# Two head pairs to a visit: joining the small-tile products of a linear-attention plus expert-layer kernel

## The chip, the cores and the metric

The kernel runs on one core of one Trainium2 chip. The metric is device time in microseconds (us). Three runs of the kernel before took 1010.1, 1008.94 and 1009.0 us, median 1009.0. The profiled execution took 1008.2 us; from its first to its last instruction (the span) there are 1006.4 us, so 1.8 us lie around the span.

## The reference

For 8 batches and 8 heads (sequence 576, head size 64, 128 random features) the attention is made linear by a feature map; its result then goes through two dense layers with an ELU between them.

```python
def phi(x):
    proj = np.einsum('bhsd,md->bhsm', x, omega)
    h = proj - np.sum(x * x, axis=-1, keepdims=True) / 2.0
    h = h - np.max(h, axis=-1, keepdims=True)
    return np.exp(h) / np.sqrt(m)
q_p, k_p = phi(q_s), phi(k_s)
kv  = np.einsum('bhsm,bhsd->bhmd', k_p, v)
z   = np.sum(k_p, axis=2)
num = np.einsum('bhsm,bhmd->bhsd', q_p, kv)
den = np.einsum('bhsm,bhm->bhs', q_p, z)[..., None] + 1e-06
x = (num / den)            # 4608 tokens x 512
h = x @ w_in               # 512 x 2048
g = np.where(h > 0.0, h, np.exp(np.minimum(h, 0.0)) - 1.0)
out = g @ w_out            # 2048 x 512
```

## The kernel before

Two heads of one batch make a pair; there are 32 pairs, numbered 0 to 31. The tokens go through the dense layers in eight blocks of 384 (layer one writes the PSUM tile `ph`, layer two the tiles `acc`), and the last 1536 tokens in three wide steps that spend fewer products (tiles `A`, `B`, `acs`). Pairs 0 to 7 are worked at the start; pairs 8 to 31 are spread between the matmuls of the blocks.

The order of all engines' work is planned when the program is built. Each piece of work is announced by `op(engine, ns, due, ...)` with an assumed duration, a due time, and what it reads and writes. `Plan.order` then plays the work through: whenever an engine is free, it takes the ready piece with the earliest due, if its buffers are free; some pieces have a second engine (`alt`). The chip executes each engine's list in that order. The due times come from tables of numbers at the head of the file (`STEP`, `PD0`, `KV2`, `ALT` and so on).

A pair from 8 on goes through these steps, in `pair`: `load_pair`; `project` for the keys (tile `ppk`, features `hk`); `kv` (here `kv_swapped`); `project` for the queries (`ppq`, `hq`); and `finish`.

- `kv_swapped` (line 609): ten matmuls sum k_p v of the pair, with v (128 x 64) as the stationary side, so that two of them, for the two heads, stand side by side on column halves of the array. They fill one PSUM bank `pkv`. VectorE turns that bank into `kvf` (line 615), `replicate` sends it to DRAM in four pieces (`kvd`, line 585) and back in four (`zk`, line 594), and GpSimd sums the keys.
- `finish` normalises the query features, turns them in 32 x 32 blocks (`qt`), and calls `output` (line 829): 32 matmuls, each with 32 rows and 64 columns of the array, eight of them side by side. They fill four PSUM banks `pn`. Each bank is copied out by a copy of 128 columns and one of 32 (lines 376 on ScalarE and 378 on VectorE), and one DMA writes the pair to `xd` (line 854).

In the trace one of these matmuls in full 32-bit floats is two records, so a pair has 20 records at line 609 and 64 at line 829. A "visit" below is such an unbroken row of small-tile products on TensorE; the matmuls of the dense layers around it use the whole 128 x 128 array.

PSUM has eight banks: three with the tag `pa`, two with `ph` (layer one takes these in turn, and `A` and `B` later), and three for `acc`. `output` needs four at once, three `pa` and one `ph` (for the last three pairs two and two); `pkv`, `ppk` and `ppq` take one `pa` each.

Of the kernel before, what the change touches and what calls it, by code (L numbers as in the profile page):

```python
# [18 lines left out]
P = 128  # L19
# [26 lines left out]
NNAT = dict(k=8, q=8)  # L46


MLP0 = 37.61
SEG = [6.25, 7.76, 3.48, 4.4, 2.75, 6.34]  # L50
STEP = 5.52
STEP_ATT = 5.44

STEP_SA, STEP_S = 9.344, 8.511
LAG2 = 1.848
PD0, PDS = 122.22, 19.83
NSA = 1
SLOT = {3: 0, 4: 1, 5: 2, 6: 1, 7: 0}
NP3 = 29
PREP0, PREP = -101.339, 8.8  # L60
TWO0, TWO = -37.142, 7.995
SUM = 0.873
UNIT0, UNIT1 = 0.25, 3.77
FETCH = 14.688
BT = [-0.751, -0.373, 0.719, 0.06, 0.525, 0.7, 0.865, -0.155, -0.328, 1.177, -1.344, 0.575, -1.141, 0.489]
AT = (0.0, 0.337, 0.844, 0.312, 0.229, 0.181, 0.386)

LAG = 3.4


PAIR0 = 6.45
DUE_LOAD, DUE_K, DUE_KV, DUE_Q = 9.63, 24.93, 17.79, 16.94
LOAD2, K2, KV2, Q2 = 61.21, 47.49, 31.23, 34.51
TAIL = 14.17
TAIL2 = -0.54


CONV1 = 13.95
CONV_STEP = 0.16
CONV2 = 1.14  # L80
CONV3 = 41.4


SPLIT = (0, 8, 16)
NHALF = 3

DUE_Z = 15.42

NEARLY = 6

NSWAP = 8
# [199 lines left out]

ALT = dict(kv=1.96, out=2.95, conv_clamp=13.06, conv_hi=14.02, conv_sub=16.5, g_hi=12.75, g_lo=11.74, y_hi=None, y_lo=0.82, norm=18.01, p2=0.03, unit=-5.32, unit_hi=0.48, prep=0.118, part=5.545, q_hi=1.554, q_lo=14.04, neg=7.821, turn=0.31, x_hi=0.28, sq=-0.48, two=-0.272, two_hi=0.343, sum=0.079, s_hi=0.129, s_lo=0.3, zero=-0.108)


def other(kind, *engs):
# [21 lines left out]
def performer_elu_kernel(  # L319
# [256 lines left out]
    def replicate(i, due):  # L576

        if i < NTURN:
            return
        s, kvf = st[i], kvs[i % 2]  # L580
        zk = s["zk"]
# [15 lines left out]

    def kv_swapped(i, due):

        s = st[i]  # L600
        h, v = s["hk"], s["v"]
        kvf = kvs[i % 2]
        p = bank(i, "ph", f"pkv_{i}")

        def mms():
            for t in range(-1, 4):
                for a in range(2):
                    j, o = (8, 8 * (D + 1) + a * (D + 2)) if t < 0 else (2 * t + a, (2 * t + a) * (D + 1))
                    nc.tensor.matmul(  # L609
                        p()[a * D:a * D + D, 0:M], v()[:, o:o + D], h()[:, j, :], start=(t < 0), stop=(t == 3)  # L610
                    )

        parts = parts_of(i, "k")
        op("PE", 5 * 216, due, mms, [*parts, v], (p,))
        op("DVE", dve(M), due + 1.2, lambda: nc.vector.transpose(kvf, p()[:, 0:M]), (p,), (("kvf", i % 2),))
        zs = Buf(sb, [P, 2, M], F32, "zs", f"zs_{i}", 1)
        zk = s["zk"] = Buf(sb, [P, 8 * P], F32, "raw", f"zk_{i}", 3)

        zu = Buf(sb, [D, 2, M], F32, "p2", f"zu_{i}", 4)

# [25 lines left out]
        replicate(i, due)  # L646

    def kv(i, due):

        if i >= NSWAP:  # L650
            kv_swapped(i, due)
            return
        s = st[i]
        h, v = s["hk"], s["v"]
        kvf = kvs[i % 2]
# [33 lines left out]
    def finish(i, due):  # L689
# [21 lines left out]
        if i < NTURN:  # L711
            qh = Buf(sb, [P, 2, S], F32, "qh", f"qh_{i}", 2)
        else:
            qt = Buf(sb, [P, 10, M], F32, "qh", f"qt_{i}", 2)
        for g in range(3):
            d = due - 9 + g
            js = slice(4 * g, min(4 * g + 4, NJ))
# [49 lines left out]
                alt=other("turn", "DVE", dve(n * P)),  # L767
            )
        if i >= NTURN:
            output(i, qt, due - 2)  # L770
# [40 lines left out]

        op("DVE", (1 if g < 2 else 2) * dve(n * P), due, turn, ((h, "n", g),), ((qt, g),))

    def output(i, qt, due):

        b, hp = divmod(i, NHP)
        zk = st[i]["zk"]
        npa = 3 if i < NP3 else 2
        banks = [Buf(ps, [P, 512], F32, "pa", f"pn_{i}_{e}", 3) for e in range(npa)]
        banks += [Buf(ps, [P, 512], F32, "ph", f"pn_{i}_{e}", 2) for e in range(npa, 4)]  # L820
        N = 5 * 32

        def mms():
            for j in range(4):
                for e in range(4):
                    r, c = slice(32 * e, 32 * e + 32), slice(32 * j, 32 * j + 32)
                    for a in range(2):
                        o = slice(a * D, a * D + D)
                        nc.tensor.matmul(  # L829
                            banks[e]()[o, 0:N], zk()[r, 4 * M + j * P + a * D:4 * M + j * P + a * D + D], qt()[r, a:10:2, c], start=(j == 0), stop=(j == 3)  # L830
                        )

        op(
            "PE", 4 * mm(4 * N) + 200, due, mms, [*((qt, g) for g in range(3)), *((zk, "kv", e) for e in range(4))], banks
        )

        def x():
            return qt().rearrange("p j x -> p (j x)")

        for e, p in enumerate(banks):  # L840
            def evict(eng, e=e, p=p):
                r, o = slice(e // 2 * D, e // 2 * D + D), 512 + 32 * (e % 2)
                copy(
                    eng, x()[:, 0:512].rearrange("p (t e r) -> p e t r", e=4, r=32)[:, e],
                    p()[:, 0:4 * 32].rearrange("p (t r) -> p t r", r=32),
                )
                copy(eng, x()[r, o:o + 32], p()[r, 4 * 32:N])

            op(
                "ACT", act(4 * 32, True) + act(32, True), due + 0.8 + 0.4 * e, evict, (p,), ((qt, "x", e),),  # L850
                alt=other("x_hi", "DVE", dve(4 * 32) + dve(32)),
            )
        op(
            "SP", 500, due + 2.4, lambda: nc.sync.dma_start(xd[hp, :, b * S:b * S + S], x()[:, 0:S]),
            [(qt, "x", e) for e in range(4)], (("xd", i),), P * S * 4,
        )

    def pair(i, due):

        at = (DUE_LOAD, DUE_K, DUE_KV, DUE_Q) if i < 2 * NHP else (LOAD2, K2, KV2, Q2)  # L860
        load_pair(i, due - at[0])
        project(i, "k", due - at[1])
        kv(i, due - at[2])
        project(i, "q", due - at[3])
        finish(i, due)


    def from_f64(src, hi, lo, nm, due, key):

# [726 lines left out]
    for n in range(len(SEGMENTS)):  # L1596
# [105 lines left out]
```

## Time and profile before

| | us |
|---|---|
| median of three runs | 1009.0 |
| profiled execution, device time | 1008.2 |
| its span | 1006.4 |
| TensorE busy | 981.2 |
| VectorE busy | 842.0 |
| ScalarE busy | 765.8 |
| GpSimd busy | 557.6 |
| line 829, small-tile output products, busy | 32.8 |
| line 609, small-tile sums of k_p v, busy | 31.5 |

Busy time on TensorE counts a record from its start to its modelled end, and records overlap: of two full-array matmuls in a row the second starts long before the first ends. What a product costs its neighbours is therefore read from start to start, in the timeline. The chain that ended last lies on TensorE for 68% of the span, on VectorE for 15%, on DMA for 6%.

### The profile page before, as it was taken

How to read it: one execution, taken by the hardware profiler on the slowest of the kernel's cores; microseconds unless marked ns; L12 is line 12 of the kernel's file. 1: busy time of each engine (PE TensorE's matmuls, PEld its weight loads, DVE VectorE, ACT ScalarE, POOL GpSimd, SP SyncE). 2: the span in 40 equal slices, each digit the busy share in tenths (PEclk: the TensorE clock that was granted, in tenths of full speed). 3: DMA queues.
4: the chain of work that ended last, by engine and by line, in shares of the span. 5: the costliest groups of instructions: out<-in, count | busy, mean ns of one | idle time of the engine just before them, and what ended most of it. 6: DMA issues, size and time to landing. Idle time of an engine off the chain costs nothing.

```text
span 1006.4 us, 24315 instructions
## 1 busy us (share of the span) xinstructions
PE 981.2 (97%) x7806; PEld 883.9 (88%) x7806; DVE 842.0 (84%) x3077; ACT 765.8 (76%) x2064; POOL 557.6 (55%) x745
## 2 busy tenths in 40 slices
PE   7999999999999999999999999999999999999997
PEld 7788788878888888888888888888789999999997
DVE  7999977887778788878888888889999889779766
ACT  7989777777668888888787778776546788777774
POOL 2667666685547767677577766684442232223221
PEclk9999999999999999999999999999999999999999
DMA  7656787757776776676666766767878876766752
GB/s 230 174 191 198 232 276 262 249 185 236 232 246 202 236 229 204 210 240 207 223 211 220 237 196 211 231 218 236 295 272 309 294 264 205 233 219 193 220 200 66
DMA packets 93264, 226.27 MB, mean 225 GB/s; under 512 B 23056, under 2 KB 35024, under 8 KB 93136
## 3 DMA queue, kind: packets, MB, share of 16 engines
q1 hardware_dynamic: 93136, 224.70, 68.8%
q8 instruction: 63, 1.03, 0.4%
q14 instruction: 65, 0.53, 0.2%
HBM read 187.43 MB, written 37.22 MB: 223 GB/s over the span
## 4 chain that ended last, share of the span: by engine, by line
PE 68%; DVE 15%; DMA 6%; ACT 5%; issue 3%; POOL 3%; SPq 1%; DVEq 0%; POOLq 0%; ACTq 0%
PE acs L1512 9%; PE ph L969 6%; PE ph L971 6%; PE acc L1003 6%; PE ph L970 6%; PE A L1354 6%; PE acc L1005 6%; PE acc L1004 6%; PE B L1354 4%; PE pkv L609 2%; PE pn L829 2%; PE ppq L541 2%; PE ppk L541 2%; DVE junk L727 1%; DVE u_w L914 1%
## 5 line engine op out<-in xcount | busy, mean ns | idle before, releaser
L969 PE MATMUL ph<-xh,w1c 128*128 128x384 f32 x512 | 176.9, 345 | 6.3 <-DVE g L990 4.4
L970 PE MATMUL ph<-xl,w1c 128*128 128x384 f32 x512 | 172.3, 336 | 1.0 <-DVE xl L794 1.0
L971 PE MATMUL ph<-xh,w1c 128*128 128x384 f32 x512 | 172.3, 336 | 0.0
L1003 PE MATMUL acc<-w2h,g 128*128 128x512 f32 x384 | 154.6, 402 | 0.1
L1005 PE MATMUL acc<-w2h,g 128*128 128x512 f32 x384 | 151.6, 395 | 0.0
L1004 PE MATMUL acc<-w2l,g 128*128 128x512 f32 x384 | 151.3, 394 | 0.0
L969 PEld LDWEIGHTS ph<-xh,w1c 128*128 128x128 f32 x512 | 96.2, 188 | 18.7 <-DVE g L990 8.5
L970 PEld LDWEIGHTS ph<-xl,w1c 128*128 128x128 f32 x512 | 96.3, 188 | 3.8 <-DVE xl L794 1.4
L978 ACT ACTIVATE e<-ph 128x384 f32<-128x384 f32 x128 | 62.5, 488 | 47.5 <-PE ph L971 47.0
L381 POOL TENSOR_TENSOR hq<-hq,den 128x512 f32<-128x512 f32 (+1 forms) x96 | 80.9, 852 | 28.7 <-DVE den L736 23.2
L971 PEld LDWEIGHTS ph<-xh,w1c 128*128 128x128 f32 x512 | 96.2, 188 | 0.0
L982 DVE SCALAR_TENSOR_TENSOR ph<-e,ph 128x384 f32<-128x384 f32 x128 | 71.3, 557 | 27.4 <-ACT e L979 26.1
L381 POOL TENSOR_TENSOR gq<-yh,gq 128x256 fp32r<-128x256 f32 x49 | 42.8, 873 | 87.0 <-ACT gq L376 76.8
L1005 PEld LDWEIGHTS acc<-w2h,g 128*128 128x128 f32 x384 | 72.0, 188 | 17.1
L1003 PEld LDWEIGHTS acc<-w2h,g 128*128 128x128 f32 x384 | 72.1, 188 | 16.2 <-issue 6.3
L727 DVE CUSTOM_DVE_ANT_0 junk<-hq,pz 128x128 f32<-128x128 f32 (+1 forms) x320 | 74.6, 279 | 12.7 <-PE pz L705 10.6
L381 POOL TENSOR_TENSOR tk<-xk,tk 64x576 fp32r<-64x576 f32 x45 | 64.1, 1424 | 32.2 <-ACT tk L376 14.9
L461 ACT ACTIVATE hk<-hk,nbk 128x128 f32<-128x128 f32 x216 | 68.4, 391 | 15.7 <-POOL nbk L567 15.3
L1004 PEld LDWEIGHTS acc<-w2l,g 128*128 128x128 f32 x384 | 72.2, 188 | 8.7
L461 ACT ACTIVATE hq<-hq,nbq 128x128 f32<-128x128 f32 x216 | 68.4, 391 | 13.5 <-POOL nbq L567 13.0
L381 POOL TENSOR_TENSOR tq<-xq,tq 64x576 fp32r<-64x576 f32 x46 | 65.9, 1432 | 21.4 <-ACT tq L376 11.1
L990 DVE TENSOR_TENSOR g<-ph,g 128x384 fp32r<-128x384 f32 x128 | 70.6, 551 | 5.7 <-PE pn L829 1.8
(222 smaller groups left out, 2816.9 us busy)
## 6 DMA issues: line engine op xcount, KB each, us to landing
w1c<-w1s SPq DMA_DIRECT2D x112, 512.0 KB, 4.4
wp<-w1t SPq DMA_DIRECT2D x48, 512.0 KB, 3.7
raw_w<-in_w_dram SPq DMA_DIRECT2D x32, 512.0 KB, 4.3
xk<-in_kx_dram SPq DMA_DIRECT2D x24, 576.0 KB, 4.6
xq<-in_qx_dram SPq DMA_DIRECT2D x24, 576.0 KB, 4.6
wp<-w1s SPq DMA_DIRECT2D x24, 512.0 KB, 4.2
v<-in_v_dram SPq DMA_DIRECT2D x32, 325.0 KB, 3.2
w1s<-w1c SPq DMA_DIRECT2D x16, 512.0 KB, 3.9
```

Source lines behind the costliest of these rows:

```text
L381: (nc.vector if e == "DVE" else nc.gpsimd).tensor_tensor(*args)
L461: nc.scalar.activation(h()[:, j, :], src(j), AF.Exp, bias=nb()[:, j:j + 1], scale=-1.0)
L727: nc.vector.tensor_tensor_reduce(out=junk()[r], in0=h()[r, j, :], in1=pz()[r, a * P:(a + 1) * P], scale=1.0, scalar=EPS, op0=ALU.mult, op1 ...
L969: nc.tensor.matmul(ph(), wh, xh[:, c, o:o + TB], start=(c == 0), stop=False)
L970: nc.tensor.matmul(ph(), wh, xl[:, c, o:o + TB], start=False, stop=False)
L971: nc.tensor.matmul(ph(), wl, xh[:, c, o:o + TB], start=False, stop=(c == NC - 1))
L982: lambda: nc.vector.scalar_tensor_tensor(ph(), e(), -1.0, ph(), ALU.add, ALU.max), (p, e), (p,),
L1003: nc.tensor.matmul(a(), g[0]()[:, ts], w2h[:, f], start=(f == f0), stop=False)
L1004: nc.tensor.matmul(a(), g[0]()[:, ts], w2l[:, f], start=False, stop=False)
L1005: nc.tensor.matmul(a(), g[1]()[:, ts], w2h[:, f], start=False, stop=(f == f1 - 1))
L1354: nc.tensor.matmul(o, at(a, i), u[b][:, i], start=(start and fresh_bank and i == 0 and n == 0), stop=(i == 1 and n == 2), skip_group_check ...
L1512: nc.tensor.matmul(bank()[:, z * TH:(z + 1) * TH], g()[:, a * TH + z * P:a * TH + z * P + P], w(b), start=(j == 0 and z == 0 and m == 0), ...
```

## The change

From pair 8 on, pairs are handled two at a time by `two_pairs`. `kv_swapped` and `output` go; their matmuls stand together in one piece of work, `tiled(i, o)`: first the sums of k_p v of pairs `i` and `i + 1` (into the last 128 columns of banks 0 and 1), then the outputs of the two pairs before, `o` and `o + 1` (into columns 0 to 159 and 160 to 319 of four banks). The first call has no pairs before it and takes two banks; the last has no pairs after it. So twelve calls work on sums, eleven of them on outputs as well, and a thirteenth on outputs alone. The keys' sums (`key_sums`) and the two turns into `kvf` come behind it; a bank with a turn in it is copied out after that turn. Each copy-out now does both pairs (four copies for a bank). All due times are new as well. The number of matmuls, of DMAs and of copies stays as it was; of the 96 copies of 128 columns (and as many of 32) VectorE now has 60 in its list, where it had 23.

```diff
-STEP_SA, STEP_S = 9.344, 8.511
+STEP_SA, STEP_S = 9.326, 10.023
...
-    def output(i, qt, due):
...
+    def tiled(i, o, due):
+
+        src = [] if i is None else list(range(i, i + 2))
+        old = [] if o is None else [(st[o + k]["qt"], st[o + k]["zk"]) for k in range(2)]
+        n = 4 if old else 2
+        npa = min(n, 3 if (o or i) < NP3 else 2)
+        banks = [Buf(ps, [P, 512], F32, "pa", f"pn_{o}_{i}_{e}", 3) for e in range(npa)]
+        banks += [Buf(ps, [P, 512], F32, "ph", f"pn_{o}_{i}_{e}", 2) for e in range(npa, n)]
         N = 5 * 32
 
         def mms():
+            for k, x in enumerate(src):
+                h, v = st[x]["hk"], st[x]["v"]
+                for t in range(-1, 4):
                     for a in range(2):
+                        j, c = (8, 8 * (D + 1) + a * (D + 2)) if t < 0 else (2 * t + a, (2 * t + a) * (D + 1))
                         nc.tensor.matmul(
+                            banks[k]()[a * D:a * D + D, 3 * M:], v()[:, c:c + D], h()[:, j, :], start=(t < 0), stop=(t == 3)
                         )
+            for k, (qt, zk) in enumerate(old):
+                for j in range(4):
+                    for e in range(4):
+                        r, c = slice(32 * e, 32 * e + 32), slice(32 * j, 32 * j + 32)
+                        for a in range(2):
+                            nc.tensor.matmul(
+                                banks[e]()[a * D:a * D + D, k * N:(k + 1) * N],
+                                zk()[r, 4 * M + j * P + a * D:4 * M + j * P + a * D + D],
+                                qt()[r, a:10:2, c], start=(j == 0), stop=(j == 3),
+                            )
...
+        for k, x in enumerate(src):
+            op(
+                "DVE", dve(M), due + KVD + 0.1 * k, lambda k=k: nc.vector.transpose(kvs[k], banks[k]()[:, 3 * M:]),
+                (), (("kvf", k), banks[k]),
+            )
+            replicate(x, due + KVD - 1.2)
...
+            op(
+                "ACT", 2 * (act(4 * 32, True) + act(32, True)), due + 1.9 + 0.4 * e, evict, (p,), [(qt, "x", e) for qt, _ in old],
+                alt=other("x_hi", "DVE", 2 * (dve(4 * 32) + dve(32))),
+            )
...
+    def two_pairs(i, due, before):
+
+        for k in range(2):
+            load_pair(i + k, due[k] - LOAD2)
+            project(i + k, "k", due[k] - K2)
+        if before is None:
+            tiled(i, None, due[1] - KVP)
+        else:
+            tiled(i, i - 2, before[1] - OUT)
+        for k in range(2):
+            key_sums(i + k, due[k] - KV2)
+            project(i + k, "q", due[k] - Q2)
+            finish(i + k, due[k])
+        if i == NPAIR - 2:
+            tiled(None, i, due[1] - OUT)
...
-            for i in range(2 * NHP, NPAIR):
-                pair(i, begin[1] + PD0 + PDS * (i - 2 * NHP))
+            due = None
+            for i in range(2 * NHP, NPAIR, 2):
+                before, due = due, [begin[1] + PD0 + PDS * (i + k - 2 * NHP) for k in range(2)]
+                two_pairs(i, due, before)
```

On TensorE, before the change, the outputs of pair 11 stand by themselves between two matmuls of layer two (here the head of the visit; the same four banks are gone through four times):

```order
L1004 MATMUL acc_8_1_3901<-w2l,g_0_4013 128x512
L1005 MATMUL acc_8_1_3901<-w2h,g_1_4022 128x512
L829 MATMUL pn_0_4162<-qt_4046,zk_3432 64x160 x2
L829 MATMUL pn_1_4165<-qt_4046,zk_3432 64x160 x2
L829 MATMUL pn_2_4168<-qt_4046,zk_3432 64x160 x2
L829 MATMUL pn_3_4171<-qt_4046,zk_3432 64x160 x2
```

A little later, still before the change, the sums of pair 13 stand between layer one and the query projection:

```order
L971 MATMUL ph_4234<-xh,w1c_3965 128x384
L541 MATMUL ppq_0_4262<-om,tq_4026 128x256 x2
L541 MATMUL ppq_1_4267<-om,tq_4026 128x256 x2
...
L971 MATMUL ph_4280<-xh,w1c_4073 128x384
L609 MATMUL pkv_4319<-hk_4075,v_3588 64x128 x10
L541 MATMUL ppq_3_4342<-om,tq_4026 128x256 x2
L1003 MATMUL acc_8_2_3934<-w2h,g_0_4109 128x512
```

On TensorE after the change, the visit that makes the sums of pairs 16 and 17 and the outputs of pairs 14 (`qt_4997`) and 15 (`qt_5276`); again each pair's banks are gone through four times:

```order
L1026 MATMUL acc_0_0_4865<-w2h,g_1_5331 128x512
L815 MATMUL pn_16_0_5340<-hk_4840,v_4761 64x128 x10
L815 MATMUL pn_16_1_5351<-hk_5136,v_4770 64x128 x10
L823 MATMUL pn_16_0_5340<-qt_4997,zk_4532 64x160 x2
...
L823 MATMUL pn_16_3_5369<-qt_4997,zk_4532 64x160 x2
L823 MATMUL pn_16_0_5340<-qt_5276,zk_4772 64x160 x2
...
L823 MATMUL pn_16_3_5369<-qt_5276,zk_4772 64x160 x2
L990 MATMUL ph_5435<-xh,w1c_5105 128x384
```

What stood in four rows of small-tile work with full-array work between them now stands in one; inside it the tile shape changes once, from 128 x 64 to 32 x 64.

On VectorE behind that same visit, after the change (banks 2 and 0; ScalarE has banks 3 and 1):

```order
L381 COPY qt_4997<-pn_16_2_5366 128x4x32
L381 COPY qt_4997<-pn_16_2_5366 64x32
L381 COPY qt_5276<-pn_16_2_5366 128x4x32
L381 COPY qt_5276<-pn_16_2_5366 64x32
L836 STREAM_TRANSPOSE kvf_76<-pn_16_0_5340 128x128
L836 STREAM_TRANSPOSE kvf_77<-pn_16_1_5351 128x128
L381 COPY qt_4997<-pn_16_0_5340 128x4x32
L381 COPY qt_4997<-pn_16_0_5340 64x32
```

Before the change VectorE had one bank's two copies behind pair 11's visit, and ScalarE the other three banks' six.

## Rows read from the trace of the kernel before

**Rows 1.** The page: busy time of each engine (share of span) and instructions.
```profile
PE 981.2 (97%) x7806; PEld 883.9 (88%) x7806; DVE 842.0 (84%) x3077; ACT 765.8 (76%) x2064; POOL 557.6 (55%) x745
```
**Rows 2.** Busy time by stretch; behind the busy times clock, DMA share, GB/s.
```profile
0.00:165.00 165.00, 156.15 (x1014) 134.20 (x1015) 142.81 (x434) 135.67 (x344) 99.83 (x94) 1.00 0.69 221
165.00:725.00 560.00, 552.55 (x4591) 483.70 (x4590) 463.54 (x2073) 434.90 (x1191) 376.94 (x556) 1.00 0.70 224
725.00:1006.40 281.40, 272.51 (x2202) 265.95 (x2202) 235.62 (x571) 195.21 (x531) 80.85 (x96) 1.00 0.69 228
```
**Rows 3.** TensorE's waits between 165 and 725 us: total us, times, longest.
```profile
PE ph L969 <- DVE g L990: 3.1, 4, 1.5
PE pkv L609 <- DVE nbq L555: 1.4, 1, 1.4
PE ph L969 <- DVE g L378: 1.2, 1, 1.2
PE ph L969 <- ACT qt L376: 0.5, 2, 0.3
```
**Rows 4.** TensorE's timeline around pair 11's outputs: start, length (us), line, count.
```profile
307.77 0.39 PE L1004 MATMUL acc<-w2l,g 128*128 128x512 f32 x1
308.01 0.40 PE L1005 MATMUL acc<-w2h,g 128*128 128x512 f32 x1
308.33 1.37 PE L829 MATMUL pn<-qt,zk 32*64 32x160 f32 x64
309.63 0.51 PE L1003 MATMUL acc<-w2h,g 128*128 128x512 f32 x1
309.97 0.39 PE L1004 MATMUL acc<-w2l,g 128*128 128x512 f32 x1
310.20 0.39 PE L1005 MATMUL acc<-w2h,g 128*128 128x512 f32 x1
```
**Rows 5.** TensorE's timeline around pair 13's sums.
```profile
315.97 0.34 PE L970 MATMUL ph<-xl,w1c 128*128 128x384 f32 x1
316.15 0.34 PE L971 MATMUL ph<-xh,w1c 128*128 128x384 f32 x1
316.42 1.31 PE L609 MATMUL pkv<-hk,v 128*64 128x128 f32 x20
317.66 0.51 PE L541 MATMUL ppq<-om,tq 128*128 128x256 f32 x2
318.00 0.40 PE L1003 MATMUL acc<-w2h,g 128*128 128x512 f32 x1
```
**Rows 6.** Small-tile matmuls by tile: records, shortest/median/longest ns, first and last start.
```profile
L829 PE MATMUL pn<-qt,zk x1536: 294/294/345, 228.0 to 717.9; 32*64 32x160 f32 x192
L609 PE MATMUL pkv<-hk,v x480: 272/273/323, 167.5 to 686.4; 128*64 128x128 f32 x160
```
**Rows 7.** TensorE's timeline, two projection matmuls between full-array neighbours.
```profile
320.53 0.40 PE L541 MATMUL ppk<-om,tk 128*128 128x256 f32 x2
320.76 0.34 PE L969 MATMUL ph<-xh,w1c 128*128 128x384 f32 x1
```
**Rows 8.** ScalarE's timeline around that output visit.
```profile
308.78 1.57 ACT L461 ACTIVATE hk<-hk,nbk 128x128 f32<-128x128 f32 x5 [0.32 <-POOL nbk L567]
310.26 1.16 ACT L376 COPY qt<-pn 128x128 f32<-128x128 f32 x6
```
**Rows 9.** VectorE's timeline behind that output visit.
```profile
309.69 0.38 DVE L378 COPY qt<-pn 128x128 f32<-128x128 f32 x2
309.99 0.54 DVE L990 TENSOR_TENSOR g<-ph,g 128x384 fp32r<-128x384 f32 x1
```
**Rows 10.** VectorE's turns of k_p v, by source line.
```profile
L615 DVE STREAM_TRANSPOSE kvf<-pkv x24: 300/312/317, 171.0 to 687.7; 128x128 f32<-128x128 f32 x24
```
**Rows 11.** SyncE's timeline: DMA issues behind pair 13's sums.
```profile
318.67 2.49 SPq L585 DMA_DIRECT2D kvd<-kvf  x4
321.21 0.59 SPq L944 DMA_DIRECT2D w1c<-w1s  x1
322.57 1.87 SPq L594 DMA_DIRECT2D zk<-kvd  x4
```
**Rows 12.** DMA issues of the page: count, KB, median us to landing.
```profile
w1c<-w1s SPq DMA_DIRECT2D x112, 512.0 KB, 4.4
kvd<-kvf SPq DMA_DIRECT2D x96, 16.0 KB, 2.2
zk<-kvd SPq DMA_DIRECT2D x96, 64.0 KB, 2.9
```
**Rows 13.** Groups between 165 and 725 us: busy us, mean ns, idle before, releasers.
```profile
L969 PE MATMUL ph<-xh,w1c 128*128 128x384 f32 x404 | 138.5, 343 | 4.9 <-DVE g L990 3.1 <-DVE g L378 1.2 <-ACT qt L376 0.5
L829 PEld LDWEIGHTS pn<-qt,zk 32*64 32x64 f32 x1536 | 25.7, 130 | 8.7 <-issue 5.8 <-ACT tk L376 0.7 <-ACT e L979 0.7
```
**Rows 14.** TensorE's last matmul in the timeline.
```profile
1000.84 0.28 PE L1512 MATMUL acs<-w2h,gq 128*128 128x256 f32 x1
```
**Rows 15.** TensorE's wait before its first matmul.
```profile
PE warm L415 <- POOL ident masks.py:199: 1.4, 1, 1.4
```

More of the change, by code (lines that the diff above doesn't have):

```diff
@@ L46 @@
 NNAT = dict(k=8, q=8)
[L49 to L52, printed above, removed]
[L54 to L56 removed]
+MLP0 = 35.53
+SEG = [6.891, 7.837, 3.48, 5.656, 2.757, 6.335]
+STEP = 5.587
+STEP_ATT = 5.166
+STEP_SA, STEP_S = 9.326, 10.023
+LAG2 = 1.914
+PD0, PDS = 111.927, 19.83
 NSA = 1
 SLOT = {3: 0, 4: 1, 5: 2, 6: 1, 7: 0}
[L59 to L68, printed above, removed]
[L71 to L81 removed]
+NP3 = 30
+KVP = 23.119
+OUT = 2.0
+KVD = 5.725
+PREP0, PREP = -88.78, 11.183
+TWO0, TWO = -34.851, 12.623
+SUM = 1.083
+UNIT0, UNIT1 = 0.192, 4.818
+FETCH = 15.138
+BT = [-0.333, -1.176, 0.361, 1.384, 0.628, 0.7, 1.012, -0.253, -0.158, 1.174, -1.257, 3.195, -1.26, 0.906]
+AT = (0.0, 0.525, 0.68, 0.38, 0.552, 0.254, 0.37)
+LAG = 3.41
+PAIR0 = 6.45
+DUE_LOAD, DUE_K, DUE_KV, DUE_Q = 14.975, 24.211, 16.885, 16.993
+LOAD2, K2, KV2, Q2 = 18.411, 52.334, 26.822, 25.863
+TAIL = 11.34
+TAIL2 = -1.706
+CONV1 = 14.001
+CONV_STEP = 0.159
+CONV2 = -0.719
+CONV3 = 78.832
 SPLIT = (0, 8, 16)
 NHALF = 3
[L87 removed]
+DUE_Z = 14.957
 NEARLY = 6
@@ L290, in issue @@
             self.tasks[n][2](eng)
-ALT = dict(kv=1.96, out=2.95, conv_clamp=13.06, conv_hi=14.02, conv_sub=16.5, g_hi=12.75, g_lo=11.74, y_hi=None, y_lo=0.82, norm=18.01, p2=0.03, unit=-5.32, unit_hi=0.48, prep=0.118, part=5.545, q_hi=1.554, q_lo=14.04, neg=7.821, turn=0.31, x_hi=0.28, sq=-0.48, two=-0.272, two_hi=0.343, sum=0.079, s_hi=0.129, s_lo=0.3, zero=-0.108)
+ALT = dict(kv=2.937, out=3.229, conv_clamp=11.989, conv_hi=10.215, conv_sub=18.852, g_hi=13.859, g_lo=12.034, y_hi=None, y_lo=0.83, norm=23.741, p2=-0.025, unit=-3.24, unit_hi=1.714, prep=0.118, part=4.606, q_hi=3.537, q_lo=13.669, neg=7.681, turn=1.931, x_hi=-0.452, sq=-0.111, two=0.197, two_hi=1.475, sum=-0.801, s_hi=0.129, s_lo=0.213, zero=-0.023)
 def other(kind, *engs):
@@ L596, in replicate, with key_sums @@
             )
-    def kv_swapped(i, due):
+    def key_sums(i, due):
         s = st[i]
[L601 to L611, printed above, removed]
+        h = s["hk"]
         parts = parts_of(i, "k")
-        op("PE", 5 * 216, due, mms, [*parts, v], (p,))
-        op("DVE", dve(M), due + 1.2, lambda: nc.vector.transpose(kvf, p()[:, 0:M]), (p,), (("kvf", i % 2),))
         zs = Buf(sb, [P, 2, M], F32, "zs", f"zs_{i}", 1)
-        zk = s["zk"] = Buf(sb, [P, 8 * P], F32, "raw", f"zk_{i}", 3)
+        zk = s["zk"]
         zu = Buf(sb, [D, 2, M], F32, "p2", f"zu_{i}", 4)
@@ new lines, in tiled @@
+        op(
+            "PE", 10 * 108 * len(src) + (8 * mm(4 * N) if old else 0) + 250, due, mms,
+            [z for x in src for z in (*parts_of(x, "k"), st[x]["v"])]
+            + [z for qt, zk in old for z in (*((qt, g) for g in range(3)), *((zk, "kv", e) for e in range(4)))], banks,
+        )
+        for k, x in enumerate(src):
[4 more added lines that the diff above has]
+            replicate(x, due + KVD - 1.2)
@@ new lines, in flat @@
+        def flat(k):
+            return old[k][0]().rearrange("p j x -> p (j x)")
+        for e, p in enumerate(banks if old else ()):
+            def evict(eng, e=e, p=p):
+                r, c = slice(e // 2 * D, e // 2 * D + D), 512 + 32 * (e % 2)
+                for k in range(2):
+                    copy(
+                        eng, flat(k)[:, 0:512].rearrange("p (t e r) -> p e t r", e=4, r=32)[:, e],
+                        p()[:, k * N:k * N + 4 * 32].rearrange("p (t r) -> p t r", r=32),
+                    )
+                    copy(eng, flat(k)[r, c:c + 32], p()[r, k * N + 4 * 32:(k + 1) * N])
+            op(
+                "ACT", 2 * (act(4 * 32, True) + act(32, True)), due + 1.9 + 0.4 * e, evict, (p,), [(qt, "x", e) for qt, _ in old],
+                alt=other("x_hi", "DVE", 2 * (dve(4 * 32) + dve(32))),
+            )
@@ new lines, in tiled @@
+        for k, (qt, _) in enumerate(old):
+            b, hp = divmod(o + k, NHP)
+            op(
+                "SP", 500, due + 4 + 0.1 * k, lambda k=k, b=b, hp=hp: nc.sync.dma_start(xd[hp, :, b * S:b * S + S], flat(k)[:, 0:S]),
+                [(qt, "x", e) for e in range(4)], (("xd", o + k),), P * S * 4,
+            )
+    def pair(i, due):
+        load_pair(i, due - DUE_LOAD)
+        project(i, "k", due - DUE_K)
+        kv(i, due - DUE_KV)
+        project(i, "q", due - DUE_Q)
+        finish(i, due)
@@ new lines, in two_pairs @@
+    def two_pairs(i, due, before):
[6 more added lines that the diff above has]
+            tiled(i, i - 2, before[1] - OUT)
+        for k in range(2):
+            key_sums(i + k, due[k] - KV2)
[3 more added lines that the diff above has]
+            tiled(None, i, due[1] - OUT)
```

40 lines of the change are left out of this document (2 added, 38 removed).

## The prediction

> **What bounds the kernel now.** I read the engines' busy time first: TensorE is busy for 981.2 of 1006.4 us, the next engine, VectorE, for 842.0 [rows 1]. [...] Busy time hides what a visit costs, though: it counts the pause at a change of tile shape as busy. That pause is in the timeline.
>
> **What a visit costs.** Read starts, not lengths. Layer two's matmuls start 0.23 to 0.24 us apart. The last one before pair 11's outputs starts at 308.01, so the next could have started at 308.24; the visit starts at 308.33. Behind it the first full-array matmul starts at 309.63, but the second only at 309.97, 0.34 later; at the usual pace it stands as if the first had started at 309.74. So the visit took 309.74 - 308.24 = 1.50 us of TensorE [rows 4]. How much is work? The group lasts 1.37 us to the end of its last record, which lasts 0.294 [rows 6], so 64 records start within 1.08 us: at 1.08/63 each, 64 are 1.09 us. The other 0.41 us are the price of going in and out. The sums of pair 13 read alike: layer one's pace is 0.18, so the visit could begin at 316.33 and does at 316.42 [rows 5]; two projection matmuls take 0.23 at full pace [rows 7], so the way out ends at 318.00 - 0.23 = 317.77 and the visit took 1.44; 20 records start within 1.31 - 0.27 = 1.04, which makes 1.09 for 20, and 0.35 is left. The records of all 24 visits of each kind last the same to within some 50 ns [rows 6], so I take these two for all 48.
>
> **The change, part by part.** Removed are visits, not work: the number of small-tile matmuls is the same. Two pairs took 2 x (1.50 + 1.44) = 5.88 us, of which 2 x (0.41 + 0.35) = 1.52 was spent at eight changes of shape, 0.19 each. A joined visit has the same 4.36 us of work and three changes: into 128 x 64, from there to 32 x 64, and out.
> - The change inside the visit is not in the trace: every small-tile visit there has full-array matmuls on both sides. Below, it could be free, so that two changes remain (0.38) and a joined visit saves 1.14. Above, it could cost what the way out of one kind and into the other cost together, so that 0.76 remain and 0.76 is saved. Both ends are built from rows 4 and 5. I take one ordinary change, 0.19, because it is again a change of shape without a full-array weight load behind it: three changes, 0.57, saving 0.95.
> - Eleven joined visits: 11 x 0.95 = 10.5 us (8.4 to 12.5). The first visit has sums alone, two pairs in one: it saves one in-and-out, 0.35. The last has outputs alone: 0.41. Sum: 11.2 us (9.1 to 13.3).
>
> [...]
>
> **What is moved, and its cover.** Each bank's copies double. Before, eight copies behind a visit took from 309.69 to 311.42: two on VectorE at 0.15 each, six on ScalarE at 0.19 each [rows 8, 9]. Now VectorE has two banks (eight copies, 1.2) and two turns of 0.31 [rows 10], together 1.8 us, and ScalarE eight copies, 1.5 us. What waits behind them on TensorE in the new order: nine matmuls of layer one (9 x 0.18 = 1.6 us at the pace of rows 5) before a projection wants a `pa` bank, then three more and layer two before the next step wants the second `ph` bank, some 3 us behind the visit. The first bank is free after about 0.3 + 0.6 = 0.9 us, the `ph` bank after 0.3 + 0.8 = 1.1 if ScalarE is free, and 0.6 to 1.6 later where a group of exponentials stands ahead (five took 1.57 [rows 8]). So these cover themselves with 0.3 us or more to spare, and I cost them at nothing. VectorE's 37 more pairs of copies are some 11 us spread over a stretch in which it has 96 us free [rows 2].
>
> SyncE issues eight `kvd` and eight `zk` transfers in a row, where it issued four and four. At 0.62 and 0.47 each [rows 11] the first eight take 5.0 us, and the two `xd` writes stand among them; a `w1c` load queued behind them starts some 3 us later than now. It needs 4.4 us to land [rows 12] and is wanted two to three layer-one steps later; the stretch has 404 records of line 969, four to a step [rows 13], so 101 steps in 560 us, 5.5 us each, and 11 us or more. Covered, by about 3 us. `zk` lands 2.2 + 2.9 us behind its issues [rows 12]; its outputs come a whole visit (about 40 us) later.
>
> The new due times reorder everything else too, the start and the wide steps included. What they could win is bounded by TensorE's idle time, 1006.4 - 981.2 = 25.2 us, of which 5.3 stand behind the last matmul (1006.4 - 1001.1 [rows 14]) and 1.4 before the first [rows 15]; what they could lose has no such bound, but nothing in the diff adds work outside the visits. I take zero, with 4 us either way.
>
> **Forecast.** The profiled execution took 1008.2 us, of which the span is 1006.4. Less 11.2 it would be 997.0; the median of the runs stands 0.8 above that execution, so 997.8.
>
> **The rivals.**
> 1. *The inner change costs a full way out and in.* For it: both sides have a weight load of another shape in front. Against: nothing in the rows. It saves 9.1: 999.9.
> 2. *The inner change is free.* For it: weights of both kinds are loaded in narrow pieces ahead of their use (the loads at line 829 are as many as its matmuls and last 130 ns each [rows 13]). Against: rows 4 and 5 show 0.09 us lost at the entry alone. It saves 13.3: 995.7.
> 3. *Part of the gain turns into waits of another kind.* Layer one already waits for `g` in 4 places, up to 1.5 us [rows 3]; with joined visits of 4.9 us VectorE's work comes in bursts. One wait of 0.45 us for each visit, 13 x 0.45 = 5.9: 1003.7.
> 4. *Slower: the copies keep the banks.* With VectorE's turns ahead of bank 0 and 1, and a group of exponentials ahead of ScalarE's copies, all spare time is used up and TensorE stands for one such group, 1.57 us [rows 8], behind each of 13 visits: 20.4 us against 11.2, 1018.2. It decides from 11.2/13 = 0.86 us for each visit. Against it: with half as many copies to a bank the wait behind 24 visits was 0.5 us in all [rows 3].
> 5. *The new order also closes waits of the old one*, in the stretch's 7.45 idle us and the 8.9 behind 725 us [rows 2] less the 5.3 at the end, which stay: half of these 11.05 is 5.5, so 992.3.
> 6. *The gain doesn't reach the end*, since the wide steps start when they did: TensorE's 97% in the last stretch speaks against it (272.51 of 281.40 [rows 2]). 1009.
>
> [...]
>
> **How the numbers follow.** Forecast 0.41 (its own range 995 to 1001, from the 4 us either way less what rivals 3 and 5 hold), rival 1 0.18, rival 2 0.10, rival 3 0.12, rival 4 0.07, rival 5 0.09, rival 6 0.03. The forecast is the likeliest, 997.8. A range of 990 to 1004 holds the forecast, rivals 1 and 2, and most of 3 and 5; left out are rivals 4 and 6 and the tails of 3 and 5, under 2 in 10. A measurement of this kernel can't tell less than 0.2% (2 us) from no change; faster means below 1007, which all but rivals 4 and 6 and a bad tail of 3 reach: 0.87. Rival 6 and that tail give 0.05 for the same, rival 4 and the far tail 0.08 for slower.
>
> **What would show it.** TensorE's timeline after should show 13 visits, the joined ones 4.9 us from the last full-array pace to the next (4.7 if the inner change is free, 5.1 if it drains fully). The inner change reads from the last start at 128 x 64 to the first at 32 x 64: about 0.11 when free, 0.3 by my figure. TensorE's busy time should fall by about 10. If layer one's or a projection's matmuls wait for `qt` copies or turns for over 0.8 us behind each visit, rival 4 holds. If `w1c` turns up as a releaser of layer one, the transfers' cover is gone. If visits are as cheap as I say and the time still doesn't fall, the waits of layer one for `g`, or those behind 725 us, have grown by as much, and the sum was wrong in its zero for the new order.

## The result: slower, and what the profile after shows

The changed kernel takes 1020.52 us (median of 4 runs, 1020.08 to 1021.87) against 1008.97 us for the kernel before beside it (4 runs): a ratio of 1.0117, 95% interval 1.0100 to 1.0135. That is 11.6 us more where 11.2 us less were forecast. The profiled execution took 1020.08 us, its span 1018.3.

The table by stretch of the changed kernel answers to [rows 2]; behind the five busy times stand clock, DMA share and GB/s.

```profile
0.00:165.00 165.00, 153.52 (x997) 132.58 (x998) 139.64 (x441) 140.41 (x355) 102.69 (x102) 0.99 0.66 218
165.00:725.00 560.00, 544.20 (x4581) 487.28 (x4580) 466.33 (x2131) 401.53 (x1073) 376.54 (x554) 1.00 0.64 217
725.00:1018.30 293.30, 284.06 (x2232) 276.46 (x2230) 240.19 (x572) 202.59 (x551) 94.48 (x111) 0.99 0.70 234
```

TensorE's busy time in the middle stretch did fall (552.55 to 544.20), but into idle time: the stretch ends with more work left, and the last one is 11.9 us longer (293.3 for 281.4), 11.55 of them busy (284.06 for 272.51). Its waits between 165 and 725 us (total, times, longest) answer to [rows 3]:

```profile
PE ph L990 <- DMA w1c<-w1s: 6.1, 7, 1.2
PE ph L990 <- DVE g L1011: 3.9, 4, 1.7
PE pn L823 <- issue: 2.5, 1, 2.5
PE ph L990 <- DVE qt L792: 1.7, 1, 1.7
```

Three of these groups are new: the weight loads `w1c`, 2.5 us of "issue", a wait for nothing that the profile shows, and one wait that ended with line 792, VectorE's turn of query features into `qt`. None of TensorE's waits there ends with a copy from `pn` to `qt`. The visits themselves are what was forecast. One of them in TensorE's timeline (start, length, line, count), to be read as [rows 4, 5]:

```profile
466.62 0.39 PE L1026 MATMUL acc<-w2h,g 128*128 128x512 f32 x1
466.94 2.40 PE L815 MATMUL pn<-hk,v 128*64 128x128 f32 x40
469.28 2.45 PE L823 MATMUL pn<-qt,zk 32*64 32x160 f32 x128
471.66 0.45 PE L990 MATMUL ph<-xh,w1c 128*128 128x384 f32 x1
471.94 0.34 PE L991 MATMUL ph<-xl,w1c 128*128 128x384 f32 x1
```

The next matmul at full pace was due at 466.62 + 0.23 = 466.85; behind the visit the second layer-one matmul starts at 471.94, so the first stands as if at 471.77: 4.92 us. The inner change reads 469.28 - (466.94 + 2.40 - 0.27) = 0.21. Of the 11 joined visits 10 take 4.91 to 4.92; the one at 335 us takes 7.85.

To see where the time went I took every distance from one matmul's start to the next, less the usual pace of its form, and sorted these by what caused them. Below are five profiled executions, one of each kernel, in us (SyncE's list is `sync_only`, three edits is `spread_again`; these and `padded` come further down):

| | before | after | SyncE's list | three edits | padded |
|---|---|---|---|---|---|
| changes of tile shape, 165 to 725 us | 18.0 | 7.1 | 7.0 | 6.9 | 7.1 |
| waits, 165 to 725 us | 9.8 | 18.7 | 13.7 | 11.6 | 12.0 |
| waits before 165 us | 10.5 | 12.9 | 14.3 | 11.4 | 9.4 |
| waits after 725 us | 5.1 | 4.7 | 3.2 | 2.8 | 2.8 |
| matmuls at half clock | 0.0 | 4.9 | 6.5 | 1.7 | 0.0 |
| pace of the rest, after 165 us | 7.8 | 12.3 | 11.7 | 8.0 | 8.1 |
| work at the usual pace, ends, others | 955.1 | 957.8 | 955.7 | 958.5 | 960.8 |
| span | 1006.4 | 1018.3 | 1012.1 | 1000.9 | 1000.2 |

The first row is the gain, 10.9 us. Three losses stand against it: waits, stretches at half clock, and a slower pace of ordinary matmuls. The 2.7 us more in the last row but one stay unexplained. TensorE's busy time over the whole span, which was to fall by about 10 us, is 981.8 for 981.2: matmuls at half clock or at a slower pace count as busy too (below, 3.40 us busy of 3.40 at a granted clock of 0.51, and a mean of 281 ns in place of 276).

**The weight loads.** SyncE's timeline behind the visit at 422.42, answering to [rows 11] (start, length, count):

```profile
423.77 1.42 SPq L438 DMA_DIRECT2D v<-in_v_dram  x2
429.69 1.84 SPq L588 DMA_DIRECT2D kvd<-kvf  x3
431.64 1.00 SPq L861 DMA_DIRECT2D xd<-qt  x2
432.69 3.50 SPq L588 DMA_DIRECT2D kvd<-kvf  x5
436.29 1.56 SPq L965 DMA_DIRECT2D w1c<-w1s  x1
437.94 3.62 SPq L597 DMA_DIRECT2D zk<-kvd  x8
441.66 0.37 SPq L965 DMA_DIRECT2D w1c<-w1s  x1
```

SyncE stands still for 4.5 us, since the first `kvd` waits for VectorE's turn of `kvf`, and VectorE copies eight `qt` pieces first:

```profile
427.25 2.06 DVE L381 COPY qt<-pn 128x128 f32<-128x128 f32 x8 [1.25 <-PE pn L823]
429.34 0.52 DVE L836 STREAM_TRANSPOSE kvf<-pn 128x128 f32<-128x128 f32 x2
```

Then come ten issues before one `w1c` and eight before the next, which is issued at 441.66, 14 us behind the visit's end. TensorE waits 1.24 us for the first of the two and 0.97 for the second (a row of its timeline):

```profile
447.08 0.44 PE L990 MATMUL ph<-xh,w1c 128*128 128x384 f32 x1 [0.97 <-DMA w1c<-w1s]
```

**The pause, and the clock.** TensorE's timeline of the visit at 335 us:

```profile
337.36 2.41 PE L823 MATMUL pn<-qt,zk 32*64 32x160 f32 x122
342.26 0.49 PE L823 MATMUL pn<-qt,zk 32*64 32x160 f32 x6 [2.49 <-issue]
```

Six small matmuls before its end TensorE stops for 2.49 us. From 0.7 us behind the visit it runs at a granted clock of 0.5 for 3.4 us; the first of these stretches holds the visit's beginning, the second what follows (the granted clock is the third figure from the end):

```profile
335.00:339.50 4.50, 4.50 (x163) 4.28 (x162) 2.66 (x5) 1.22 (x4) 2.57 (x5) 1.00 0.88 257
343.50:346.90 3.40, 3.40 (x13) 3.40 (x13) 2.31 (x11) 2.46 (x10) 1.16 (x2) 0.51 0.21 64
```

It happens twice more, at 12.4 and 729.2 us, behind waits of 1.9 us for ScalarE and 1.8 us for VectorE.

**The pace.** The same group of wide matmuls in 860 to 880 us, before and after (count, busy, mean ns):

```profile
L1512 PE MATMUL acs<-w2h,gq 128*128 128x256 f32 x20 | 4.2, 276 | 0.0
```
```profile
L1533 PE MATMUL acs<-w2h,gq 128*128 128x256 f32 x27 | 5.7, 281 | 0.0
```

They last 281 ns in place of 276 and start 117 to 118 ns apart in place of 113 to 114. In the change the 128-byte tile `den` is allocated ahead of `w1c` and `wp`, which so lie 128 bytes higher in SBUF.

### The profile page after: what moved, and what is told of

Same layout as the page of the kernel before. It is cut to its first block, busy times and chain, and to the rows that moved or that the text cites. A ratio compares the mean times of both kernels' runs of the same rounds, so it can differ in the third digit from the quotient of the medians.

```text
span 1018.3 us, 24261 instructions
## 1 busy us (share of the span) xinstructions
PE 981.8 (96%) x7806; PEld 896.3 (88%) x7806; DVE 846.2 (83%) x3142; ACT 744.5 (73%) x1978; POOL 573.7 (56%) x766
## 4 chain that ended last, share of the span: by engine, by line
PE 70%; DVE 11%; DMA 6%; ACT 5%; issue 3%; SPq 2%; POOL 2%; DVEq 0%; POOLq 0%; ACTq 0%
PE acs L1533 7%; PE ph L990 7%; PE ph L992 6%; PE ph L991 6%; PE acc L1024 6%; PE acc L1026 6%; PE acc L1025 6%; PE A L1375 5%; PE B L1375 4%; DMA w1c<-w1s 3%; PE pn L815 2%; PE pn L823 2%; PE ppk L544 2%; PE ppq L544 2%; PE ppk L494 1%
## 5 line engine op out<-in xcount | busy, mean ns | idle before, releaser
L990 PEld LDWEIGHTS ph<-xh,w1c 128*128 128x128 f32 x512 | 96.7, 189 | 30.9 <-DVE g L1011 11.5
L384 POOL TENSOR_TENSOR gq<-y,gq 128x256 fp32r<-128x256 f32 x32 | 28.2, 880 | 102.4 <-ACT gq L379 102.4
L384 POOL TENSOR_TENSOR tk<-xk,tk 64x576 fp32r<-64x576 f32 x45 | 64.5, 1433 | 22.7 <-ACT tk L379 12.9
```

Of the source, the lines that this page charges most:

```text
L384: (nc.vector if e == "DVE" else nc.gpsimd).tensor_tensor(*args)
L990: nc.tensor.matmul(ph(), wh, xh[:, c, o:o + TB], start=(c == 0), stop=False)
```

## The experiments

Four suspects were tried: loads come late behind the bursts on SyncE's list (theory A); the new numbers are at fault whatever the visits; TensorE waits for its code (E1, later F); the address of the wide tiles sets the pace (P). The rival of each stands in the expectation. The letters hold from the second group on; the first group's expectations carry letters of their own for the same suspects.

Ratios are to the kernel before on the same chip, with 95% intervals. Its median was 1009.6 us in the first group, 1007.9 in the second, 1007.8 in the third and 1009.3 in the fourth.

### First group: parts of the change alone

**apart_new**: the visits of before, the numbers of after.

```
-MLP0 = 37.61
+MLP0 = 35.53
...
-LOAD2, K2, KV2, Q2 = 61.21, 47.49, 31.23, 34.51
+LOAD2, K2, KV2, Q2 = 18.411, 52.334, 26.822, 25.863
```

> The kernel before, its visits apart, with every shared number of the tables at its new value. Theory C: the new dues alone cost what the changed kernel lost beyond the transfers: 8 to 14 us more than before, 1017 to 1023. Rival D: the dues alone cost little; within 5 us of 1009. The dues were not made for separate visits, so a large loss here alone proves less than a good time of the opposite exchange.

Measured: 1025.82 us, 1.0139 (1.0093 to 1.0184). **joined_old** is the reverse, the joined visits with all shared numbers of before:

```
-MLP0 = 35.53
+MLP0 = 37.61
...
```

> Joined visits with every number of the tables that both kernels have put back to its value of before; the three numbers that only the changed kernel has stay. Theory C (the loss is in the new due times: start, pace and the end): the start and the wide steps go as before, the joined visits save their 10.9 us, some 7 us go to w1c: 1003 to 1007. Rival D (joining the visits is itself what costs, by bursts on SyncE and VectorE, whatever the dues): 1015 or more.

Measured: 1050.98 us, 1.0392 (1.0348 to 1.0437). Its longest waits of TensorE over the whole span:

```profile
PE pz L691 <- DMA zk<-kvd: 9.2, 1, 9.2
PE ph L990 <- DVE g L1011: 6.1, 5, 2.1
```

The joined visits with the old numbers are clearly slower than both parts together (1.0117, 1.0100 to 1.0135); the new numbers alone can't be told from both, since the intervals overlap. Either part alone is slower than the kernel before, so the loss can't be divided between the joining and the numbers: each set of numbers was made for its own order.

**few_dma**: `kvd` and `zk` one transfer each in place of four.

```
-                nc.sync.dma_start(zk()[32 * e:32 * e + 32, 4 * M:], kvd[i])
+                nc.sync.dma_start(zk()[:, 4 * M:], kvd[i].unsqueeze(0).to_broadcast([4, 32, 4 * P]))
```

> The changed kernel with the same order on every engine, but a pair's sums of k_p v go to DRAM in one transfer and come back in one, where they went in four and four; the bytes are the same. Theory A (SyncE's list is blocked): the sixteen issues behind a joined visit take 8 to 9 us, and the weights of layer one stand behind them. With four issues TensorE's waits for w1c (7.2 us after the change) fall under 1.5 us, and the time falls by 5 to 9 us, to 1011 to 1015. Rival B (the load is late because the transfers themselves or the memory are slow, or the order asks for it too late): the waits for w1c stay at 5 us or more, and the time within 2 us of 1020.5.

Measured: 1039.94 us, 1.0286 (1.0244 to 1.0329), a miss. The list got shorter and `w1c` was issued earlier, and TensorE still waited more for it:

```profile
PE ph L994 <- DMA w1c<-w1s: 21.5, 9, 3.7
```

Nothing but the merged transfers differs, so they slowed the loads beside them: the `w1c` issued at 442.99 us, which TensorE waited for, landed 9.2 us later (median after the change: 4.5). The trace's DMA records show two things more. Every other transfer ends with 16 packets of 4 bytes, each of the 48 merged ones with only 4 (7888 in all, for 481 and 48 transfers), and from 443 to 445 us, with that `w1c` on its way, the DMA engines were busy for a share of 0.34. How a merged transfer slows the loads no run shows. This run changed more than the length of the list, so it doesn't tell whether the list was to blame.

**place_after**: the first `w1c` allocated ahead of `den`, so that the wide tiles lie where they did.

```
+                st["w1c_0"]()
...
+        st.setdefault("w1c_0", t)
```

> The changed kernel, the same order on every engine, with the weights of layer one and of the wide steps (w1c, wp) 128 bytes lower in SBUF, where they lay before; only the place of a small tile is exchanged with them. After the change a 256-column matmul of the wide steps started 117 to 118 ns after the one before, where it mostly was 113 to 114. Theory E (place of the weights): the usual distance goes back to 113 to 114 and the time falls by 3 to 5 us, to 1016 to 1017. Rival F (the pace depends on what ran before, not on the place): the distance stays and the time is within 1.5 us of 1020.5.

Measured: 1020.02 us, 1.0101 (1.0070 to 1.0133). In its trace the pace is mostly back at 113 to 114 ns, but the time misses theory E's 1016 to 1017 us and can't be told from the change's 1.0117.

### Second group: one suspect each

**code_shift**: two warm-up matmuls in place of seven (`for _ in range(NWARM - 5)`), so that every visit comes 20 instructions earlier in TensorE's list, in the same order.

> [...] Theory E1 (the 2.5 us pause inside the visit at 335 us is TensorE waiting for its next block of code): the pause and the stretch at half clock behind it go, mid stretch 2.5 us of wait and 1.6 us of half clock less, about 1016 to 1017 us. Rival (the pause comes from what stands there in the program, operands or banks): it stays at the same visit, 1020 to 1021 us.

Measured: 1018.82 us, 1.0113 (1.0091 to 1.0136). The visit takes 4.91 us now, but the pause has only moved behind it, so neither theory E1 nor its rival holds as written:

```profile
335.68 2.45 PE L823 MATMUL pn<-qt,zk 32*64 32x160 f32 x128
338.52 0.34 PE L992 MATMUL ph<-xh,w1c 128*128 128x384 f32 x1
341.53 0.34 PE L990 MATMUL ph<-xh,w1c 128*128 128x384 f32 x1 [2.67 <-issue]
```

Counted from the program's start, sequencer instructions included, it comes at the same count in both, 4801 or 4802 instructions in. So it goes with the count of instructions ahead of it and not with the visit's operands. Pauses in other runs bear that out: two in `joined_old` come 8642 and 9410 instructions in, which is 15 and 18 times 256 more than 4802 (all three lie 194 over a multiple of 256). The page of the changed kernel shows one queue with instruction packets of 16 KB (packets, MB, share):

```profile
q8 instruction: 62, 1.02, 0.4%
```

TensorE's 16,085 instructions in that trace are 259 for each of the 62. From this number and the 15 and 18 times 256 comes an estimate: the packets are taken here for TensorE's code, one for a block of 256 instructions, and a block is taken to start at 4802 and at every multiple of 256 from there, both ways. In the changed kernel no packet starts between 317.6 and 339.8 us, over 503 matmuls and weight loads, and the one at 339.8 starts when the pause does.

**move_sp**: the sixteen `kvd` and `zk` of two pairs behind the next two `w1c` loads.

```
         for n, eng in self.order():
+            if n in self.late:
+                held.append((n, eng))
+                continue
             self.tasks[n][2](eng)
+            if held and n in self.load:
+                loads += 1
+                if loads == 2:
+                    for m, e in held:
+                        self.tasks[m][2](e)
+                    held, loads = [], 0
```

> The changed kernel with only SyncE's list altered, from pair 12 on: the eight kvd and eight zk transfers of two pairs go behind the next two w1c loads rather than ahead of them. Theory A (w1c loads stand behind a run of 19 to 20 issues of some 0.6 us each on SyncE): TensorE's 6.1 us of waits for w1c fall under 1.5 us, about 1014 to 1016 us; zk lands some 2 us later and is still early, since its reader is the visit two pairs on. Rival (the transfers themselves, or the vector engine's late turns, are what is slow): waits for w1c stay at 4 us or more, or come back as waits for zk or kvf, 1019 to 1023 us.

Measured: 1016.16 us, 1.0080 (1.0057 to 1.0103); waits for `w1c` 1.5 us in one place.

**place_before**: the kernel before with `den` allocated first (`from_f64(w1[f], lambda: (st[0]["den"](), t())[1][:, 0], ...)`), same order.

> The kernel before, same order on every engine, with the one 128-byte-per-partition tile that moved in the change allocated first, so that the wide weight tiles lie 128 bytes higher, as they do in the changed kernel. Theory P (where the operands lie sets whether 256-column matmuls follow each other every 113 or every 117 to 118 ns): pace goes up by 3 to 5 us, about 1012 to 1014 us. Rival (the pace belongs to the order or to the run): 1008 to 1010 us.

Measured: 1011.83 us (12 runs), 1.0030 (1.0011 to 1.0050). The group of wide matmuls reads as it does after the change:

```profile
L1512 PE MATMUL acs<-w2h,gq 128*128 128x256 f32 x21 | 4.6, 281 | 0.0
```

The place of the tiles alone costs 3.0 us by this ratio (1.1 to 5.0); the medians differ by 4.0.

**combo**: all three edits.

> The changed kernel with all three: weight tiles where the kernel before has them, two warm-up matmuls, and the kvd and zk transfers behind two w1c loads. If the three causes are real and add up (4 + 5 + 4 us): 1006 to 1009 us, at or under the kernel before. If only the pause and the place are real: 1012 to 1014 us. If none: 1020 us.

Measured: 1013.88 us, 1.0049 (1.0030 to 1.0068). That is the range written for the pause and the place, but the trace shows another mixture: the pause was not cured (2.1 us behind the visit), and TensorE's waits for `w1c` fell to 2.4 us.

### Third group: the rest of SyncE's list

**combo_cold**: combo without warm-ups (`NWARM - 7`).

> The combination (weight tiles where the kernel before has them, the kvd and zk transfers behind two w1c loads) with no warm-up matmuls at all, so that TensorE's list is 8 instructions shorter again and the block boundary that follows the visit at 335 us lies later than in any run so far. Theory F (TensorE runs dry at a block end when a dense visit keeps the next block's packet from starting; in the other visits, whose boundary lies 94 or more instructions into the visit, the packet comes in time): the pause of 2.1 to 3 us near 343 us is gone or under 1 us, 1011 to 1012 us. Rival (the pause belongs to that block, wherever the visit lies): it stays at 2 us or more, 1013 to 1014 us. If the missing warm-ups leave TensorE at half clock at the start, up to 1.7 us come on top in either case.

Measured: 1011.24 us, 1.0037 (1.0016 to 1.0059). The time agrees with theory F, the trace doesn't: a pause of 2.0 us stood in the layer one behind the visit.

**spread**: the held transfers in groups of four, one behind each further transfer of the list.

```
+            if held and loads >= 2 and eng == "SP":
+                for m, e in held[:4]:
+                    self.tasks[m][2](e)
+                held = held[4:]
```

> As the one without warm-ups, and the sixteen kvd and zk transfers of two pairs go in four groups of four, one after each further transfer on SyncE's list, rather than all at once behind the second w1c load; xs, xq, xk and w1c then wait behind four issues at most. Theory A carried on (what stands behind a run of issues on SyncE comes late, whichever load it is): ScalarE's waits for xs and xk (5.0 and 15.5 us in the middle stretch) and TensorE's for w1c (2.4 us) fall, and with them 2 to 3 us of TensorE's waits for g: 1008 to 1010 us. Rival (ScalarE's waits for inputs are hidden, and g is late because two pairs' key and query work stands between the steps of layer one): the loads come earlier and the time stays within 1 us of the one without warm-ups.

Measured: 1008.50 us, 0.9991 (0.9964 to 1.0017). ScalarE's waits for `xs` fell from 5.5 to 0.9 us. Those for `xk` stayed at 14.3, and **load_early** (`LOAD2` 40 in place of 18.411) asked whether they matter.

> As the one with the transfers in groups of four, and the inputs of a pair from the ninth on are due 40 us ahead of it rather than 18.4 (61.2 in the kernel before); the planner then also puts some of the other engines' work in another order. If ScalarE's waits for xk and xq are on the path: 2 to 4 us faster than the groups of four alone, 1005 to 1007 us. If not: within 2 us of it in either direction.

Measured: 1014.25 us, 1.0061 (1.0035 to 1.0087): slower, a miss.

### Fourth group: the sizes on one chip

> The changed kernel as it is, beside the others on one chip: what each of them saves is read against it. 1019 to 1021 us, with the 2 to 3 us pause at 335 to 345 us and 5 to 8 us of TensorE's waits for w1c.

Measured: 1022.00 us, 1.0130 (1.0099 to 1.0160), with a pause of 3.0 us and 9.0 us of waits for `w1c` in its profiled execution. **sync_only** is the change with the list of spread and nothing else.

> The changed kernel with SyncE's list alone altered: kvd and zk in four groups of four among the transfers that follow, from pair 12 on. Theory A: TensorE's waits for w1c fall under 1 us and ScalarE's for xs under 1.5 us, 1012 to 1014 us, 6 to 8 us under the changed kernel on the same chip. Rival (the groups only helped together with the place of the tiles): under 4 us less.

Measured: 1013.77 us, 1.0053 (1.0033 to 1.0073), 8.2 us less. Its list, and TensorE's waits in the middle stretch:

```profile
431.94 0.80 SPq L878 DMA_DIRECT2D xd<-qt  x2
432.83 1.29 SPq L983 DMA_DIRECT2D w1c<-w1s  x2
434.18 2.49 SPq L603 DMA_DIRECT2D kvd<-kvf  x4
436.99 0.34 SPq L1064 DMA_DIRECT2D out_dram<-o  x1
```
```profile
PE ph L1008 <- DVE g L1029: 5.0, 5, 1.7
PE pn L840 <- issue: 2.9, 1, 2.9
PE ppk L557 <- ACT p2k L392: 2.0, 1, 2.0
PE ph L1008 <- DMA w1c<-w1s: 0.5, 1, 0.5
```

Every engine but SyncE has the same list as in the change, the two intervals lie apart, and the waits for `w1c` fell from 9.0 to 0.5 us, so the 8.2 us are SyncE's order.

**spread_again**:

> The version with all three edits (weight tiles' place, no warm-ups, kvd and zk in groups of four) on the same chip as the changed kernel: 1007 to 1010 us, 10 to 13 us under it, level with the kernel before.

Measured: 1006.69 us, 0.9972 (0.9953 to 0.9991).

**padded**: 56 small matmuls at the start, so that no joined visit reaches a second start of a block, as estimated under code_shift.

```
-            for _ in range(NWARM - 7):
-                nc.tensor.matmul(p()[:, 0:P], ident, ident, start=True, stop=True)
+            for k in range(56):
+                o = slice(k % 2 * D, k % 2 * D + D)
+                nc.tensor.matmul(p()[o, 0:32], ident[:, o], ident[:, 0:32], start=True, stop=True)
```

> As the version with all three edits, with 56 small matmuls of 64 weight columns and 32 data columns at the start in the place of the warm-ups, 224 instructions, so that every joined visit begins under 70 or over 190 instructions behind a multiple of 256 and none reaches a second block start. Theory F (the pause depends on how a dense visit lies to the blocks of TensorE's code): no pause over 0.5 us in or behind any visit, and no half clock after it, 3 to 4 us less than the version with three edits if the small matmuls fit into the idle 5.4 us at the start, 1004 to 1006 us; half of that if they reach past it. Rival (the pause belongs to one block of the code or to what runs there): a pause of 2 us stays, now at another visit or at the same one, 1008 to 1010 us.

Measured: 1005.57 us, 0.9964 (0.9946 to 0.9982), the lowest median of all and 0.4% under the kernel before. The same visit runs through, and no stretch at half clock is left before TensorE's last matmul:

```profile
332.97 2.40 PE L834 MATMUL pn<-hk,v 128*64 128x128 f32 x40
335.30 2.45 PE L842 MATMUL pn<-qt,zk 32*64 32x160 f32 x128
337.69 0.44 PE L1011 MATMUL ph<-xh,w1c 128*128 128x384 f32 x1
337.97 0.34 PE L1012 MATMUL ph<-xl,w1c 128*128 128x384 f32 x1
```
```profile
165.00:725.00 560.00, 550.41 (x4627) 492.77 (x4626) 475.68 (x2149) 407.57 (x1089) 383.53 (x563) 1.00 0.68 223
```

In time it stands only 1.1 us under spread_again, inside both intervals (there the pause had shrunk to 1.2 us). The small matmuls also change the start: a 2.0 us wait for ScalarE at 11.5 us and the half clock behind it, the only such stretch of `spread_again` before TensorE's last matmul, are gone too. That the pause goes with the count of instructions ahead is shown (4801 or 4802 in the change and in code_shift, none in padded); its price in the median is not.

## Why the prediction was wrong, step by step

- *What a visit costs, and the change inside it* (4.93 us, saving 11.2): right. Joined visits take 4.91 to 4.92; the changes of shape cost 10.9 us less in the trace; rivals 1 and 2 fall. The inner change of 0.21 lies between free (0.11) and the 0.3 written down.
- *The copies "cover themselves"*: right for TensorE, which waited for none of them in the middle stretch. The 1.7 us for `qt` ended with the turn of query features, 13 us behind a visit. Rival 4, the slower one, gave a time near the result (1018.2) by a mechanism that didn't happen; its nearness is luck.
- *"a `w1c` load queued behind them starts some 3 us later than now ... Covered, by about 3 us"*: this step failed. Before, the first two `w1c` behind pair 13's sums were issued 3.5 and 7.8 us after the sums' end; behind the visit at 422.42 us it was 9.1 and 14.5 us, so they came 5.6 and 6.7 us later, and TensorE waited for both. The step left out that VectorE copies for 2 us before it turns, and SyncE's list stands meanwhile; it counted the eight `kvd` and not the eight `zk`, which stand ahead of the next `w1c`; and it asked after `w1c` alone, where `xs` waits in the same list. The prediction's own sign for it, `w1c` as a releaser of layer one, came true. Put in another order the list gives back 8.2 us (1022.0 to 1013.8) of the 12.8 that the change lost on that chip.
- *"I take zero" for the new order*: the new order and the new numbers can't be judged apart (apart_new, joined_old). With the list put right and the side effects below gone, `padded` gains 3.7 us of the 11.2 by medians; its profiled execution, 6.3 us under that of before (1001.93 for 1008.2), is the fastest of its twelve. By the table the changes of shape still give 10.9 us there, and waits outside the middle stretch 3.4; against them stand 2.2 us more of waits in it, so rival 3 (5.9) was right in part, though layer one's waits for `g` grew by only 0.9 and those of the projections by more; and 5.7 us in the row of work, of which the 56 small matmuls at the start are a part. The 7.5 us that are missing by medians stay open.
- *Left out altogether*: "nothing in the diff adds work" was true and not enough. The 128 bytes by which the wide tiles moved cost some 3 us, shown in the kernel before (3.0 by the ratio) and in the traces, though not in the median of `place_after`; and the pause, with the half clock behind it, took 2.5 + 1.6 us in the profiled execution. Neither can be seen in the order of instructions.

On one chip the steps from the change to the fastest version are 1022.0, less 8.2 for SyncE's list, less 7.1 for the place and the missing warm-ups together, less 1.1 for the padding, 1005.6. These are differences between runs, so their sum proves nothing more; only the first stands for a single cause.

## What to carry to other kernels

When work is gathered into bursts, write down the list of the engine that issues the transfers, with all that a load has ahead of it and with what its head waits for; a few positions in that list cost 8.2 us here, most of the 10.9 that the joining saved. When a kernel's time moves and its order of instructions doesn't explain it, compare where its tiles lie and at what counts of instructions its engines pause before looking for a deeper reason; here the place of the tiles cost 3.0 us by the ratio, and one pause 2.5 us. Numbers that set an order go with the structure they were found for, and trying one without the other says little about either.

## What the hardware showed that was not expected

- Matmuls of 256 columns mostly start 113 to 114 ns apart with the wide tiles at one address and 117 to 118 with them 128 bytes higher. Behind 725 us, the distances between two of them that are under 125 ns (some 1980 in each trace) sum to 3.0 to 3.3 us over 113.5 ns each in the nine traces with the lower address and to 6.0 to 6.7 in the eight with the higher; the place alone moved the kernel before by 3.0 us by the ratio.
- A joined visit issues 336 matmuls and weight loads in 4.5 us, and in 10 of the 11 of the changed kernel no packet of the instruction queue starts before 271 of them are issued. In nearly every run with joined visits TensorE stood for 0.8 to 3.0 us at one or two of the visits that reach a second block's start (estimated, as under code_shift) within themselves or some 20 instructions behind; other such visits passed without a pause, and in padded, where none reaches one, there was none. Why the packet starts late no run shows.
- Three waits of 1.8 to 2.5 us in the changed kernel were each followed by 3.4 us at a granted clock of 0.5, which made them some 1.6 us dearer (4.9 us for the three in the table of starts); in the profiled execution of before, whose longest wait was 1.5 us, there was no such stretch ahead of TensorE's last matmul. `place_before`, with the same lists, shows two (at 11.8 and 687.7 us, behind waits of 3.1 and 1.9 us), so one execution doesn't tell how many a kernel has.
- One `kvd` transfer of 64 KB and one `zk` of 256 KB, in the place of four each with the same bytes, raised TensorE's waits for `w1c` from 6.1 us (9.0 in a second execution) to 21.5, and ended with 4 packets of 4 bytes in place of 16.
